# Batch 0 of an attention-and-feed-forward kernel: value projections ahead of the products, copies on two engines, a second block put off

## The chip, the cores and the metric

The kernel runs on one core of a Trainium2 chip. The metric is the device time of one execution in microseconds (us). Runs of this kernel on one core show a granted TensorE clock of 0.998 to 1.0. A ratio is computed as the mean time of one kernel's runs over that of the other's of the same rounds, so it is not quite the ratio of the medians that are quoted.

## The reference, cut to what matters

```python
# q, k, v: 8 batches x 8 heads x 1024 positions x 64; E, F: 64 x 1024
k_proj = einsum('ks,bhsd->bhkd', E, k)
v_proj = einsum('ks,bhsd->bhkd', F, v)
attn   = softmax(q @ k_proj^T / sqrt(64))          # over 64 projected keys
x      = (attn @ v_proj), heads side by side       # 8192 tokens x 512
h      = x @ w_in                                  # 512 -> 2048
out    = (h * clip(h + 3, 0, 6) / 6) @ w_out       # 2048 -> 512
```

The feed-forward part holds nearly all the matmul work: 2048 matmuls of 128*128 by 512 columns. Attention of batch b + 1 is woven into the feed-forward work of batch b. Batch 0 has nothing to hide behind: its attention is the head of the program.

## The kernel before

Heads go in pairs (`j`, four of them); tokens in two blocks (`t`, 512 each). Everything below is batch 0.

```python
def values_out(self, ps, hs, second=None, copies=(0, 1)):   # projected values: PSUM -> SBUF, twice
    src = ps[KP:].rearrange("p (h d) -> p h d", d=D)
    for a in copies:        # a = 0: rows 0-63, read by block 0; a = 1: rows 64-127, read by block 1
        (second if a and second else nc.vector.tensor_copy)(self.vp[a * KP:(a + 1) * KP, hs, :], src)

def quads(self, stationary, j, alloc, ts=range(NB)):        # sums and products: 64*64 tiles of the array
    tiles = {t: alloc() for t in ts}
    for t in ts:
        for a in range(2):
            r, c = t * KP, a * D                            # block t uses row half t
            nc.tensor.matmul(tiles[t][c:c + D]..., stationary(r, 2 * j + a), self.aT[j][r:r + KP, :, a, :], ...)
    return tiles

def by_pairs(self):
    ...
    for j in range(KO):                                     # the first loop
        keys(j)
        if j > 0: self.scores(j - 1, pmm)                   # ends in two exponentials on ScalarE
        busy(1)                                             # filler: one matmul nobody reads
        self.keys_transposed(2 * j, 2)
        self.q_out(j, self.q_transpose(j, pat))
        busy(1)
        if j > 0:
            ts = range(NB) if j == 1 else (0,)              # pair 0: both blocks
            den = self.sums(j - 1, pmm, ts)
            lns = {t: self.log(den[t]) for t in ts}         # 1 / sum = exp(-log(sum)), on ScalarE
            recs[j - 1, 0] = reciprocal(lns[0], opool, "o_sb")
            if j == 1:
                recs[0, 1] = self.inverse(lns[1])
            busy(1)
    self.scores(KO - 1, pmm)
    rest = []
    for j in range(KO):                                     # the tail
        copy = vals(j)                                      # eight projection matmuls
        copy(0)
        if j == 0: copy(1)
        else: rest.append(copy)
        av = self.values(j, pat, range(NB) if j == 0 else (0,))
        self.scaled(j, 0, av[0], recs[j, 0])
        busy(1)
        if j == 0:
            self.scaled(0, 1, av[1], recs[0, 1])
            den = self.sums(KO - 1, pmm, (0,))
            ...
            busy(1)
    for copy in rest: copy(1)
    busy(2)

def second_block(self):                  # one step after each feed-forward group
    for j in range(1, KO):
        for _ in range(3): yield
        den = self.sums(j, pat, (1,))[1]                    # "a visit"
        av = self.values(j, pat, (1,))[1]
        rec = self.inverse(self.log(den))
        yield
        self.scaled(j, 1, av, rec)
```

The softmax here doesn't subtract the row's maximum and nothing guards it: scores larger than these inputs give would overflow.

Of the kernel before, what the change touches and what calls it, by code (L numbers as in the profile page):

```python
# [15 lines left out]
def kernel(  # L16
# [11 lines left out]
    nc = tc.nc  # L28
# [7 lines left out]
    KO = d_model // P  # L36
    FO = d_ff // P
    TOK = 512
    NB = S // TOK
# [19 lines left out]
    opool = ctx.enter_context(tc.tile_pool(name="o", bufs=4))  # L59
# [5 lines left out]
    def pmm():  # L65
        return ps_mm.tile([P, TOK], f32, tag="mm", name="mm")

    def pat():
        return ps_at.tile([P, TOK], f32, tag="at", name="at")
# [11 lines left out]
    def busy(n):  # L81
        ps = pmm()
        for _ in range(n):
            nc.tensor.matmul(ps, ones[:, :P], ones, start=True, stop=True)  # L84
# [57 lines left out]
    class Attention:  # L142
# [15 lines left out]
            for a in range(2):  # L158
                (second if a and second else nc.vector.tensor_copy)(self.kp[:, hs, a, :], src)  # L159

        def values_out(self, ps, hs, second=None, copies=(0, 1)):
            src = ps[KP:].rearrange("p (h d) -> p h d", d=D)
            for a in copies:
                (second if a and second else nc.vector.tensor_copy)(self.vp[a * KP:(a + 1) * KP, hs, :], src)  # L164

        def keys_transposed(self, h0, n):
# [50 lines left out]
        def sums(self, j, alloc, ts=range(NB)):  # L217
            return self.quads(lambda r, h: ones[r:r + KP, :D], j, alloc, ts)
# [15 lines left out]
            nc.vector.tensor_mul(self.xT[:, j, t, :], av, rec)  # L234



        def by_pairs(self):
            def pair(j):
                return slice(2 * j, 2 * j + 2)  # L240

            def keys(j):
                pk = pat()[:, :P]
                for so in range(SO):
                    self.project(pk, 0, pair(j), so)
                self.keys_out(pk, pair(j))

            def vals(j):
                pv = pat()[:, :P]
                for so in range(SO):  # L250
                    self.project(pv, 1, pair(j), so)
                return lambda a: self.values_out(pv, pair(j), copies=(a,))

            def reciprocal(ln, pool, tag):
                rec = pool.tile([P, TOK], f32, tag=tag, name=tag)
                nc.scalar.activation(rec, ln, AF.Exp, scale=-1.0)
                return rec


            recs = {}  # L260
            for j in range(KO):
                keys(j)
                if j > 0:
                    self.scores(j - 1, pmm)
                busy(1)
                self.keys_transposed(2 * j, 2)
                self.q_out(j, self.q_transpose(j, pat))
                busy(1)
                if j > 0:
                    ts = range(NB) if j == 1 else (0,)  # L270
                    den = self.sums(j - 1, pmm, ts)
                    lns = {t: self.log(den[t]) for t in ts}
                    recs[j - 1, 0] = reciprocal(lns[0], opool, "o_sb")
                    if j == 1:
                        recs[0, 1] = self.inverse(lns[1])
                    busy(1)
            self.scores(KO - 1, pmm)
            rest = []
            for j in range(KO):
                copy = vals(j)  # L280
                copy(0)
                if j == 0:
                    copy(1)
                else:
                    rest.append(copy)
                av = self.values(j, pat, range(NB) if j == 0 else (0,))
                self.scaled(j, 0, av[0], recs[j, 0])
                busy(1)
                if j == 0:
                    self.scaled(0, 1, av[1], recs[0, 1])  # L290
                    den = self.sums(KO - 1, pmm, (0,))
                    recs[KO - 1, 0] = reciprocal(self.log(den[0]), opool, "o_sb")
                    busy(1)
            for copy in rest:
                copy(1)
            busy(2)


        def second_block(self):
            for j in range(1, KO):  # L300
                for _ in range(3):
                    yield
                den = self.sums(j, pat, (1,))[1]
                av = self.values(j, pat, (1,))[1]
# [3 lines that stand above are left out]
# [97 lines left out]
    second = first.second_block()  # L405
# [69 lines left out]
```

## Time and profile before

| | before |
|---|---|
| median of six runs | 522.02 us (521.97 to 522.26) |
| first key projection | 8.00 us |
| first feed-forward group of batch 0 | 27.79 us |
| first projection of batch 1 | 56.61 us |
| second-block visits | 3 |

In the lines of profiles below, PE is TensorE, PEld its weight loads, DVE is VectorE, ACT is ScalarE and POOL is GpSimd; a q behind the name is the engine's sequencer, and L373 is line 373 of that kernel's file. `mm` and `at` are PSUM tiles, `aT` the exponentials of a pair, `vp` its projected values, `xT` the scaled attention output. A bracket such as [0.70 <-ACT aT L203] says that the engine stood idle for 0.70 us before this line, and that ScalarE's exponentials ended the wait.

The last three rows are read from the instructions in order of time. The first key projection starts when the first loads (E and F) have landed and been turned; that moment wanders between 7.5 and 8.1 us from run to run, so later I subtract it. The difference "first projection of batch 1 minus first key projection" is the length of the part that the change touches: 56.61 - 8.00 = 48.61 us here.

### The profile page before, as it was taken

The numbers are of one execution on the slowest core, as the hardware profiler recorded it, in microseconds if no ns is written. First come the engines' busy times: TensorE is split into PE (matmuls) and PEld (weight loads), VectorE is DVE, ScalarE is ACT, GpSimd is POOL, SyncE is SP. The second block draws the span as 40 slices with busy tenths as digits, with TensorE's granted clock in tenths as the row PEclk, the third lists the DMA queues.
The fourth block names the chain that finished last, engine by engine and source line by source line (L and its number), as shares of the span: only waits on it lengthen the run. The fifth ranks groups of instructions, "written<-read, shape, count | busy, mean of one in ns | idle before, by whom it ended". The sixth has DMA issues, their size and how long they took to land.

```text
span 520.4 us, 7264 instructions
## 1 busy us (share of the span) xinstructions
PE 506.5 (97%) x2804; PEld 225.7 (43%) x2856; DVE 239.5 (46%) x379; ACT 284.0 (55%) x517; POOL 35.4 (7%) x53
## 2 busy tenths in 40 slices
PE   7899999999999999999999999999999999999997
PEld 3444444444444444444444444444444444444443
DVE  3478536444363453554454354534525544444420
ACT  2667485675446654568437664466635664444431
POOL 7520001000020000200002000200000000000000
PEclk9999999999999999999999999999999999999999
DMA  9999993993049611795119831298111110111112
GB/s 168 203 207 207 207 180 108 185 150 96 27 76 210 144 42 40 120 195 121 42 30 166 175 85 42 61 206 169 42 40 32 40 42 24 38 40 43 40 42 81
DMA packets 67443, 54.21 MB, mean 104 GB/s; under 512 B 29776, under 2 KB 59216, under 8 KB 67408
## 3 DMA queue, kind: packets, MB, share of 16 engines
q0 software_dynamic: 29856, 29.36, 35.0%
q1 hardware_dynamic: 37328, 23.99, 17.3%
q10 hardware_dynamic: 224, 0.39, 0.3%
q8 instruction: 22, 0.36, 0.3%
q14 instruction: 13, 0.11, 0.1%
HBM read 59.24 MB, written 16.78 MB: 146 GB/s over the span
## 4 chain that ended last, share of the span: by engine, by line
PE 94%; ACT 1%; DVE 1%; issue 1%; DMA 1%; DVEq 0%; ACTq 0%
PE mm L373 43%; PE mm L382 41%; PE at L212 4%; PE at L152 3%; PE at L198 1%; DMA ef_f<-in_F_dram 1%; PE mm L84 1%; PE at L182 1%; ACT aT L203 0%; PE mm L212 0%; DVE vp L164 0%; ACT ln L225 0%; PE mm L198 0%; DVE kp L159 0%; ACT rec L230 0%
## 5 line engine op out<-in xcount | busy, mean ns | idle before, releaser
L377 DVE SCALAR_TENSOR_TENSOR g<-r,mm 128x512 bf16<-128x512 f32 x256 | 173.2, 685 | 218.3 <-ACT r L376 218.1
L373 PE MATMUL mm<-xT,w_in_sb 128*128 128x512 bf16 x1000 | 233.1, 379 | 2.6 <-issue 1.9
L382 PE MATMUL mm<-w_out_sb,g 128*128 128x512 bf16 x999 | 230.1, 379 | 1.5 <-issue 0.3
L376 ACT ACTIVATE r<-mm 128x512 f32<-128x512 f32 x256 | 152.3, 603 | 66.1 <-PE mm L373 64.7
L373 PEld LDWEIGHTS <-w_in_sb 128*128 128x128 bf16 x1024 | 96.9, 98 | 125.5 <-issue 14.1
L382 PEld LDWEIGHTS <-g 128*128 128x128 bf16 x1024 | 99.0, 98 | 119.3 <-issue 2.2
L396 ACT COPY o_sb<-mm 128x512 f32<-128x512 f32 x63 | 36.9, 586 | 147.7 <-PE mm L382 144.8
L234 DVE TENSOR_TENSOR xT<-at,rec 128x512 bf16<-128x512 f32 x52 | 35.5, 683 | 15.4 <-ACT rec L230 15.4
L230 ACT ACTIVATE rec<-ln 128x512 f32<-128x512 f32 x60 | 38.0, 640 | 0.1
L225 ACT ACTIVATE ln<-at 128x512 f32<-128x512 f32 x59 | 32.6, 617 | 2.3 <-PE at L212 2.3
L203 ACT ACTIVATE aT<-at 128x512 bf16<-128x512 f32 x56 | 29.2, 612 | 0.9 <-PE at L198 0.9
L338 POOL COPY mark<-kT 1x1 bf16<-1x1 bf16 x5 | 0.9, 176 | 277.9 <-DMA kT<-kp 277.9
L152 PE MATMUL at<-k,ef_t 128*64 128x512 bf16 (+1 forms) x88 | 15.9, 324 | 0.3 <-issue 0.3
L152 PE MATMUL at<-v,ef_t 128*64 128x512 bf16 (+1 forms) x88 | 15.9, 324 | 0.0
L212 PE MATMUL at<-aT,vp 64*64 64x512 bf16 x112 | 12.6, 379 | 1.5 <-DVE vp L164 1.5
L152 PEld LDWEIGHTS <-ef_t 128*64 128x64 bf16 x176 | 9.5, 109 | 9.6 <-issue 4.7
L212 PE MATMUL at<-aT,ones 64*64 64x512 bf16 x118 | 12.7, 400 | 0.0
L164 DVE CAST vp<-at 64x512 bf16<-64x512 f32 (+1 forms) x21 | 11.2, 541 | 2.8 <-PE at L152 1.6
L84 PE MATMUL mm<-ones 128*128 128x512 bf16 x29 | 10.4, 440 | 1.6 <-DVE ones L77 1.5
L159 DVE CAST kp<-at 64x512 bf16<-64x512 f32 (+1 forms) x21 | 10.2, 523 | 3.1 <-PE at L152 3.0
L212 PEld LDWEIGHTS <-ones 64*64 64x64 bf16 x128 | 4.0, 103 | 14.8 <-issue 14.0
L189 DVE COPY qTp<-at 128x1024 bf16<-128x1024 bf16 x8 | 5.5, 691 | 7.5 <-PE at L182 7.5
(44 smaller groups left out, 100.4 us busy)
## 6 DMA issues: line engine op xcount, KB each, us to landing
out_dram<-o_sb SPq DMA_DIRECT2D x63, 256.0 KB, 2.0
q<-in_q_dram POOLq DMA_DIRECT2D x7, 1024.0 KB, 9.8
k<-in_k_dram POOLq DMA_DIRECT2D x7, 1024.0 KB, 15.3
v<-in_v_dram POOLq DMA_DIRECT2D x7, 1024.0 KB, 20.2
w_out_sb<-in_moe_w_out_dram POOLq DMA_DIRECT2D x4, 512.0 KB, 27.6
w_in_sb<-in_moe_w_in_dram POOLq DMA_DIRECT2D x3, 512.0 KB, 13.2
k<-in_k_dram POOLq DMA_DIRECT2D x4, 256.0 KB, 6.6
q<-in_q_dram POOLq DMA_DIRECT2D x4, 256.0 KB, 7.1
```

Source lines behind the costliest of these rows:

```text
L84: nc.tensor.matmul(ps, ones[:, :P], ones, start=True, stop=True)
L152: nc.tensor.matmul(ps[e * KP:(e + 1) * KP], ef_t[e][:, so, :], kqv[self.b]["kv"[e]][:, hs, so, :], start=(so == 0), stop=(so == SO - 1))
L203: nc.scalar.activation(self.aT[j][:, r].rearrange("p a n -> p (a n)"), tiles[r], AF.Exp, scale=scale)
L212: nc.tensor.matmul(tiles[t][c:c + D].rearrange("p (r n) -> p r n", r=2), stationary(r, 2 * j + a), self.aT[j][r:r + KP, :, a, :], start=Tr ...
L225: nc.scalar.activation(ln, den, AF.Ln)
L230: nc.scalar.activation(rec, ln, AF.Exp, scale=-1.0)
L234: nc.vector.tensor_mul(self.xT[:, j, t, :], av, rec)
L373: nc.tensor.matmul(h_ps, w_in_sb[:, ko, fo * P:(fo + 1) * P], xT[:, ko, t, :], start=(ko == 0), stop=(ko == KO - 1))
L376: nc.scalar.activation(r, h_ps, AF.Relu, bias=0.5, scale=1.0 / 6.0)
L377: nc.vector.scalar_tensor_tensor(g[:, fo, :], r, 1.0, h_ps, op0=ALU.min, op1=ALU.mult)
L382: nc.tensor.matmul(o_ps, g[:, fo, c * P:(c + 1) * P], w_out_sb[:, fo, :], start=(fo == 0), stop=(fo == FO - 1))
L396: nc.scalar.copy(o_sb, o_ps)
```

## The change

The intent: keep TensorE from standing still while a projection's copy is made, by issuing the next projection first; take the second copy off VectorE; and get pair 0's second block out of the head, into the feed-forward phase where the other pairs' second blocks already are.

```diff
             for j in range(KO):
                 keys(j)
 ...
                 if j > 0:
-                    ts = range(NB) if j == 1 else (0,)
-                    den = self.sums(j - 1, pmm, ts)
-                    lns = {t: self.log(den[t]) for t in ts}
-                    recs[j - 1, 0] = reciprocal(lns[0], opool, "o_sb")
-                    if j == 1:
-                        recs[0, 1] = self.inverse(lns[1])
+                    sums(j - 1)                      # block 0 only
                     busy(1)
             self.scores(KO - 1, pmm)
-            ... (the tail loop shown above)
+            vals(0)                                  # copies: VectorE, then ScalarE
+            vals(1)
+            sums(KO - 1)
+            products(0)                              # block 0 only, then its scaling
+            busy(1)
+            vals(2)
+            products(1)
+            busy(1)
+            products(2)
+            vals(3)
+            busy(1)
+            products(3)
+            busy(2)
 
         def second_block(self):
-            for j in range(1, KO):
-                for _ in range(3):
+            for j in range(KO):
+                for _ in range(2):
                     yield
```

More of the change, by code (lines that the diff above doesn't have):

```diff
@@ L159, in keys_out, with values_out @@
                 (second if a and second else nc.vector.tensor_copy)(self.kp[:, hs, a, :], src)
-        def values_out(self, ps, hs, second=None, copies=(0, 1)):
+        def values_out(self, ps, hs, second=None):
             src = ps[KP:].rearrange("p (h d) -> p h d", d=D)
-            for a in copies:
+            for a in range(2):
                 (second if a and second else nc.vector.tensor_copy)(self.vp[a * KP:(a + 1) * KP, hs, :], src)
@@ L251, in vals @@
                     self.project(pv, 1, pair(j), so)
-                return lambda a: self.values_out(pv, pair(j), copies=(a,))
+                self.values_out(pv, pair(j), nc.scalar.copy)
             def reciprocal(ln, pool, tag):
@@ L257, in reciprocal, with sums, products @@
                 return rec
-            recs = {}
+            one = (0,)
+            recs, avs = {}, {}
+            def sums(j):
+                ln = self.log(self.sums(j, pmm, one)[0])
+                recs[j] = reciprocal(ln, opool, "o_sb")
+            def products(j):
+                self.scaled(j, 0, self.values(j, pat, one)[0], recs[j])
             for j in range(KO):
@@ L269, in by_pairs @@
                 if j > 0:
-                    ts = range(NB) if j == 1 else (0,)
-                    den = self.sums(j - 1, pmm, ts)
-                    lns = {t: self.log(den[t]) for t in ts}
-                    recs[j - 1, 0] = reciprocal(lns[0], opool, "o_sb")
-                    if j == 1:
-                        recs[0, 1] = self.inverse(lns[1])
+                    sums(j - 1)
                     busy(1)
             self.scores(KO - 1, pmm)
-            rest = []
-            for j in range(KO):
-                copy = vals(j)
-                copy(0)
-                if j == 0:
-                    copy(1)
-                else:
-                    rest.append(copy)
-                av = self.values(j, pat, range(NB) if j == 0 else (0,))
-                self.scaled(j, 0, av[0], recs[j, 0])
-                busy(1)
-                if j == 0:
-                    self.scaled(0, 1, av[1], recs[0, 1])
-                    den = self.sums(KO - 1, pmm, (0,))
-                    recs[KO - 1, 0] = reciprocal(self.log(den[0]), opool, "o_sb")
-                    busy(1)
-            for copy in rest:
-                copy(1)
+            vals(0)
[10 more added lines that the diff above has]
+            products(3)
             busy(2)
         def second_block(self):
-            for j in range(1, KO):
-                for _ in range(3):
+            for j in range(KO):
+                for _ in range(2):
                     yield
```

## The prediction

> **What bounds the kernel now.** I read the shares of the engines first, then the chain that ended last, then the first 80 us in order of time, then who waited for whom.
>
> ```profile
> PE 506.5 (97%) x2804; PEld 225.7 (43%) x2856; DVE 239.5 (46%) x379; ACT 284.0 (55%) x517; POOL 35.4 (7%) x53
> PE 94%; ACT 1%; DVE 1%; issue 1%; DMA 1%; DVEq 0%; ACTq 0%
> ```
>
> TensorE is busy for 97% of the span and is 94% of the chain. From 27.79 us on, where batch 0's first feed-forward group starts, its waits add up to only a few us, and they hang on its own order of work. So the time is the start of that group, plus all matmul work after it. The change touches both: it reorders the head before 27.79 us and moves one matmul slot behind it. All gain must come from TensorE's idle time and filler before 27.79 us.
>
> Two stretches of that head carry the argument (columns: start us, duration us, engine, line, operation; in brackets idle time before it and what ended it):
>
> ```profile
> 12.37 0.41 PE L212 MATMUL mm<-aT,ones 64*64 64x512 bf16 x4
> 12.81 1.09 ACT L225 ACTIVATE ln<-mm 128x512 f32<-128x512 f32 x2 [0.50 <-PE mm L212]
> 13.78 0.63 ACT L256 ACTIVATE o_sb<-ln 128x512 f32<-128x512 f32 x1
> 14.30 0.63 ACT L230 ACTIVATE rec<-ln 128x512 f32<-128x512 f32 x1
> 14.82 1.08 ACT L203 ACTIVATE aT<-mm 128x512 bf16<-128x512 f32 x2
> 15.96 0.40 PE L212 MATMUL mm<-aT,ones 64*64 64x512 bf16 x2 [0.70 <-ACT aT L203]
> ```
>
> Pair 0 takes logarithm and reciprocal for both token blocks (four activations). The exponentials of pair 1, whose scores TensorE started at 13.59, wait behind them until 14.82, and TensorE then stands still for 0.70 us.
>
> ```profile
> 19.43 0.41 PE L198 MATMUL mm<-qTp,kT 64*64 64x256 bf16 x8 [0.25 <-DVE qTp L189]
> 20.38 1.06 ACT L203 ACTIVATE aT<-mm 128x512 bf16<-128x512 f32 x2
> 20.79 0.73 PE L212 MATMUL at<-aT,vp 64*64 64x512 bf16 x4 [0.39 <-DVE vp L164]
> 22.43 0.63 PE L152 MATMUL at<-v,ef_t 128*64 128x128 bf16 x8
> 23.10 0.29 DVE L164 CAST vp<-at 64x128 bf16<-64x128 f32 x1 [0.51 <-PE at L152]
> 23.45 0.40 PE L212 MATMUL at<-aT,vp 64*64 64x512 bf16 x2 [0.39 <-DVE vp L164]
> 27.79 3.62 PE L373 MATMUL mm<-xT,w_in_sb 128*128 128x512 bf16 x16
> PE at L212 <- DVE vp L164: 1.5, 4, 0.4
> ```
>
> In the tail each pair is projection, copy, product in strict sequence. Projection start to product start is 1.02 us, though the projection's eight matmuls free TensorE after 0.56 us (keys at 16.61, scores at 17.17). So 0.46 us is lost four times; the wait list shows 0.39 of each.
>
> The second block's price, after 27.79 us:
>
> ```profile
> 31.34 0.40 PE L212 MATMUL at<-aT,ones 64*64 64x512 bf16 x2
> 31.58 0.38 PE L212 MATMUL at<-aT,vp 64*64 64x512 bf16 x2
> 31.89 3.63 PE L373 MATMUL mm<-xT,w_in_sb 128*128 128x512 bf16 x16
> ```
>
> The starts 27.79, 31.89, 36.00 and 40.11 lie 4.10 to 4.11 us apart, and sixteen matmuls at 0.216 are 3.46. One second-block visit costs TensorE 0.64 us.
>
> **What the Trainium skill says.** "TensorEngine Tiling (Array Packing)", Key Properties: tiles of the array run independently, and changing the tiling mode drains TensorE. The trace agrees: four 64*64 matmuls of pair 0's sums took 0.41 us, two took 0.40, so dropping block 1's sums there saves TensorE nothing, and doing them later costs a new visit. "TensorE: Matmul & The Clock Gate", the engine queue depths in Part 1: ScalarE and VectorE are strict FIFOs. The trace agrees: pair 1's ready exponentials stood behind four activations. "PSUM — Partial Sum Buffer", Terms: two engines on one bank and quadrant at once are a collision, even both reading. The trace shows the program keeping to that: batch 1's key copies on the two engines run one after the other (VectorE 60.77 for 0.68, ScalarE only at 61.48, released by VectorE). So "two engines" will not make the pair of copies parallel; it only takes the second one off VectorE. "ScalarE: Activation LUTs", What ACT_TABLE_LOAD costs: 186 ns + 0.833 ns per element for an activation with immediates. For 512 elements that gives 613 ns, and the trace has 580 to 600; for the new copy of 128 elements it gives 0.29 us, an estimate.
>
> **The change part by part.**
>
> *1. Block 1 of pair 0 leaves the first loop.* TensorE: nothing (0.41 against 0.40). ScalarE loses one log and one reciprocal. Recomputed: log at 12.81, reciprocal 0.62 later (19.22 to 19.84 in the pair-3 case) at 13.43, ScalarE free 0.54 later at 13.97. Scores started at 13.59, and exponentials can follow 0.45 later (17.18 to 17.63), at 14.04. They end 1.08 later at 15.12, and pair 1's sums can start at 15.18. TensorE gets there at 14.88 + 0.31 = 15.19. So 15.20 instead of 15.96: **gain 0.76**. The next step (sums to sums 2.81 us) stays as it is, so pair 3's scores start at 18.67 and their exponentials end at 21.44 - 0.76 = 20.68.
>
> *2. The tail, step by step* (pitches from the trace: projection 0.56, products to filler 0.33, filler to next 0.32, sums to products in the same mode 0.24):
> - projection 0 at 19.01, projection 1 at 19.57, done 20.13. No copy is waited for.
> - sums of pair 3: need both exponentials, end 20.68, so 20.74. **New wait 0.61.**
> - products 0 at 20.98, filler 21.31, projection 2 at 21.63, products 1 at 22.19, filler 22.52, products 2 at 22.83 (copy of pair 2 on VectorE 22.30 to 22.59, then 0.06: in time), projection 3 at 23.16, filler 23.72, free at 24.04.
> - products 3: projection 3 done at 23.83, but VectorE is in the scaling of pair 2 (start 23.36 behind pair 1's, 0.66 each), so the copy runs 24.02 to 24.31 and products 3 start at 24.37. **Remaining wait 0.33.**
> - two fillers: 0.33 + 2 x 0.216 = 0.77 to the first group, at 25.14. The last scaling ends about 25.6; the matmul that reads it is the fourth, at 25.79.
>
> Tail before: 27.79 - 19.77 = 8.02. After: 25.14 - 19.01 = 6.13. **Gain 1.89.** Its terms: waits 1.84 become 0.94 (0.90); block 1 of pair 0's products, which came one after the other (0.66 to the filler), leaves 0.33; one single filler and one of the last three go (about 0.54); the rest is cheaper mode changes.
>
> *3. Copies.* Products of block 0 read only the half that VectorE copies. ScalarE's copies stand behind the pair 3 exponentials (two from 20.68) and end before its logarithm can start at 21.18 or just after; the reciprocal is needed only near 24.9. The three late copies that VectorE had at 28.03 lay beside matmuls and are worth nothing.
>
> *4. Second block.* Four visits instead of three: **loss 0.64**. Every three groups instead of four: ScalarE needs 3 x 0.54 + 1.2 = 2.8 us and VectorE 4 x 0.66 = 2.6 us of each 3 x 0.864 + 0.64 = 3.23 us, so neither becomes the bound.
>
> Sum: 522.11 - 0.76 - 1.89 + 0.64 = **520.1 us**.
>
> **The rivals.**
> - *Value loads become the bound.* The table of DMA issues gives 11.1, 11.1, 11.0 and 11.0 us to landing; from issues at 7.57, 8.31, 9.63 and 10.88 the four pairs land at 18.67, 19.41, 20.63 and 21.88. My times of need are 19.01, 19.57, 21.63 and 23.16. All arrive before, the second by only 0.16, and behind it comes a 0.61 wait which would swallow that. If they came 1 us late, the time would be 520.6 to 521. Nothing in the change reorders loads, so I give this little.
> - *The earlier start is lost to a later load.* Weight pieces land at 23.26, 24.63, 27.15, 29.70 and 32.2; the fifth group would need the third piece at 29.2. The last piece of the second weights lands at 29.94 + 27.6 = 57.5; its use moves from 62.8 to 60.8. Batch 2's values land at 42.86 + 31.8 = 74.7, needed at 81.0 - 2.0 = 79.0. Nothing becomes late; if something did, 522.1.
> - *Second-block visits crowd ScalarE.* After a visit the next activation is about 0.35 us late and has caught up two groups later; three groups suffice by my sum. If PSUM backed up at each visit, add 0.3 x 4: 521.3.
> - *The new order is a pure win without the exponential wait*, if ScalarE reached pair 3 sooner: at most 0.6 better, 519.5. Against it speaks the strict order of log, reciprocal, exponentials on ScalarE.
>
> **Range and chances.** The three terms have errors of perhaps 0.3 each from pitches read to 0.05 us, and runs spread by 0.3 (521.97 to 522.26). Losses are likelier than extra gains, as every new order of engines can uncover a wait. So 519.5 to 521.0. 2% is 10.4 us, far more than the head's whole idle time; within 2% has 0.987, faster 0.008, slower 0.005.
>
> **What would show it.** Right: no 0.70 us idle before pair 1's sums near 15.2; a wait of about 0.6 on the exponentials before pair 3's sums at 20.7; one wait near 0.3 on the value copy before the last products; first group near 25.1; four second-block visits about 3.2 us apart; the rest shifted by 2.0 us. Wrong: TensorE waiting on a value load, the first products waiting for ScalarE's copy, or matmul gaps between second-block visits.

## More of the kernel before

A warning on one number. This is the costliest TensorE group of the page (columns: line, engine, operation, tiles, shapes and count; then busy time and mean ns; then idle time before it and its releaser):

```profile
L373 PE MATMUL mm<-xT,w_in_sb 128*128 128x512 bf16 x1000 | 233.1, 379 | 2.6 <-issue 1.9
```

The program has 1024 of these matmuls, not 1000: some records are missing from this trace, and each gap shows as idle time that ended by itself ("issue"). So the share of TensorE is a lower bound, and small "issue" gaps are not waits.

## The result, and the profile after

The changed kernel takes 520.14 us (median of six runs, 520.02 to 520.19) against 522.02 us: 1.88 us less. The ratio is 0.9963 with a 95% interval from 0.9950 to 0.9976: a real gain of 0.4%, within 2%. The prediction was 520.1.

The page of the changed kernel: shares of the engines, the chain that ended last, and the costliest TensorE group (the feed-forward line is now line 370):

```profile
PE 511.5 (99%) x2854; PEld 225.5 (44%) x2854; DVE 238.6 (46%) x375; ACT 285.2 (55%) x521; POOL 35.4 (7%) x53
PE 96%; DVE 1%; ACT 1%; issue 0%; DVEq 0%; ACTq 0%
L370 PE MATMUL mm<-xT,w_in_sb 128*128 128x512 bf16 x1024 | 236.6, 379 | 0.0
```

TensorE's busy time seems to have risen by 5 us in a kernel that does less. It has not: this trace has all 1024 records, and the 2.6 us of idle time ahead of that group are gone with the gaps. Shares of busy time cannot measure this change; start times can.

The first loop around pair 1 (in order of time, columns as in the prediction):

```profile
12.14 0.40 PE L212 MATMUL mm<-aT,ones 64*64 64x512 bf16 x2 
12.59 0.60 ACT L225 ACTIVATE ln<-mm 128x512 f32<-128x512 f32 x1 [0.50 <-PE mm L212]
13.21 0.63 ACT L255 ACTIVATE o_sb<-ln 128x512 f32<-128x512 f32 x1 
13.82 1.08 ACT L203 ACTIVATE aT<-mm 128x512 bf16<-128x512 f32 x2 
14.96 0.40 PE L212 MATMUL mm<-aT,ones 64*64 64x512 bf16 x2 
```

One logarithm and one reciprocal stand ahead of the exponentials, and pair 1's sums start without a wait. On the clock of the first key projection (7.77 here, 8.00 before) they come at 7.19 instead of 7.96.

The tail:

```profile
18.77 1.11 PE L152 MATMUL at<-v,ef_t 128*64 128x128 bf16 x16 
19.38 1.06 ACT L203 ACTIVATE aT<-mm 128x512 bf16<-128x512 f32 x2 
20.50 0.40 PE L212 MATMUL mm<-aT,ones 64*64 64x512 bf16 x2 [0.61 <-ACT aT L203]
...
22.45 1.35 DVE L234 TENSOR_TENSOR xT<-at,o_sb 128x512 bf16<-128x512 f32 x2 
...
23.82 0.29 DVE L164 CAST vp<-at 64x128 bf16<-64x128 f32 x1 
24.15 0.26 ACT L164 CAST vp<-at 64x128 bf16<-64x128 f32 x1 [1.53 <-DVE vp L164]
24.17 0.40 PE L212 MATMUL at<-aT,vp 64*64 64x512 bf16 x2 [0.30 <-DVE vp L164]
24.95 2.75 PE L370 MATMUL mm<-xT,w_in_sb 128*128 128x512 bf16 x12 
```

Sixteen projection matmuls (pairs 0 and 1) run on almost without a stop (0.04 us, see the rivals below); the exponentials of pair 3 then make TensorE wait 0.61 us; two scalings keep VectorE until 23.8, and the last products wait 0.30 us for the copy behind them. From first projection to first group the tail is 24.95 - 18.77 = 6.18 us, against 8.02 before. ScalarE's copy of a pair does wait for VectorE's copy of the same tile, and the products do not wait for it.

The first second-block visit after it:

```profile
27.63 0.40 PE L212 MATMUL at<-aT,ones 64*64 64x512 bf16 x2 
27.87 0.38 PE L212 MATMUL at<-aT,vp 64*64 64x512 bf16 x2 
28.19 2.76 PE L370 MATMUL mm<-xT,w_in_sb 128*128 128x512 bf16 x12 
```

Visits start at 27.63, 30.88, 34.13 and 37.37, 3.24 to 3.25 us apart, with twelve matmuls of 0.216 us (2.59) between: 0.65 us a visit, four times. From there on every output copy of the changed kernel lies 2.17 to 2.18 us ahead of the kernel before, to the last one. 0.23 of that is the wandering start; 1.95 is the change.

### The profile page after: what moved, and what is told of

It is laid out like the page before. It is cut to its first block, busy times and chain, and to the rows that moved or that the text cites. A ratio compares the mean times of both kernels' runs of the same rounds, so it can differ in the third digit from the quotient of the medians.

```text
span 518.3 us, 7310 instructions
## 1 busy us (share of the span) xinstructions
PE 511.5 (99%) x2854; PEld 225.5 (44%) x2854; DVE 238.6 (46%) x375; ACT 285.2 (55%) x521; POOL 35.4 (7%) x53
## 4 chain that ended last, share of the span: by engine, by line
PE 96%; DVE 1%; ACT 1%; issue 0%; DVEq 0%; ACTq 0%
PE mm L370 44%; PE mm L379 42%; PE at L212 3%; PE at L152 3%; PE mm L84 2%; PE at L198 1%; PE at L182 1%; PE mm L212 0%; ACT aT L203 0%; DVE xT L234 0%; PE mm L198 0%; DVE kp L159 0%; DVE vp L164 0%; ACT ln L225 0%; PE at L169 0%
## 5 line engine op out<-in xcount | busy, mean ns | idle before, releaser
L370 PE MATMUL mm<-xT,w_in_sb 128*128 128x512 bf16 x1024 | 236.6, 379 | 0.0
L84 PE MATMUL mm<-ones 128*128 128x512 bf16 x30 | 11.7, 477 | 1.5 <-DVE ones L77 1.5
```

What stands on the lines that cost most here:

```text
L84: nc.tensor.matmul(ps, ones[:, :P], ones, start=True, stop=True)
L370: nc.tensor.matmul(h_ps, w_in_sb[:, ko, fo * P:(fo + 1) * P], xT[:, ko, t, :], start=(ko == 0), stop=(ko == KO - 1))
```

## The experiments

Eleven runs, all correct, five rounds each (four runs for combined_recip) beside the kernel before on the same chip (whose median there was 522.01 to 522.05). The table gives the median of the runs, and from the profiled run the "touched part" (first projection of batch 1 minus first key projection, 48.61 before). The two columns of differences need not agree to better than about 0.2 us, because the median also carries the wandering start; in free_block and combined, the end of the program adds some 0.35 us, as told there.

Every kernel of the table is within 2% of the kernel before. The 95% intervals of the ratios reach some 0.7 us to either side. Those of late_recip (0.9978 to 1.0003) and put_off_only (0.9980 to 1.0007) include 1, all others lie below it. So the gains of these two, and every difference of a few tenths between two of the new kernels, rest on the start times in the profiled runs and not on the times alone.

| kernel | median us | less than before | touched part us | less than before |
|---|---|---|---|---|
| changed kernel | 520.14 | 1.88 | 54.43 - 7.77 = 46.66 | 1.95 |
| late_recip | 521.45 | 0.56 | 55.87 - 7.78 = 48.09 | 0.52 |
| put_off_only | 521.60 | 0.41 | 56.30 - 8.08 = 48.22 | 0.39 |
| order_only | 520.52 | 1.49 | 54.91 - 7.77 = 47.14 | 1.47 |
| copies_vector | 520.35 | 1.66 | 54.77 - 7.93 = 46.84 | 1.77 |
| no_fillers | 519.62 | 2.43 | 53.79 - 7.53 = 46.26 | 2.35 |
| sums_later | 519.65 | 2.40 | 53.94 - 7.51 = 46.43 | 2.18 |
| free_block | 519.83 | 2.22 | 53.85 - 7.78 = 46.07 | 2.54 |
| free_block_again | 519.79 | 2.23 | 53.87 - 7.79 = 46.08 | 2.53 |
| combined | 518.72 | 3.30 | 52.73 - 7.78 = 44.95 | 3.66 |
| combined_padded | 518.33 | 3.71 | 52.72 - 7.89 = 44.83 | 3.78 |
| combined_recip | 517.82 | 4.22 | 52.10 - 7.55 = 44.55 | 4.06 |

The theory throughout is that of the prediction: ScalarE's strict order makes the wait in the first loop, copies make the waits in the tail, a visit costs TensorE 0.64 us. The main rivals are that one of the two parts (put-off or new order) makes the whole gain, and that the second engine matters.

### late_recip: one reciprocal moved in the kernel before

```diff
                     self.scores(j - 1, pmm)
+                    if j == 2:
+                        recs[0, 1] = self.inverse(ln01)
 ...
-                        recs[0, 1] = self.inverse(lns[1])
+                        ln01 = lns[1]
```

> The kernel before, with one activation moved: the reciprocal of pair 0's second block is issued behind pair 1's exponentials instead of ahead of them; nothing else changes. Theory (ScalarE's strict order causes the 0.70 us wait of pair 1's sums): exponentials start when the first reciprocal frees ScalarE, 0.50 us earlier than before (14.32 instead of 14.82), sums 0.50 us earlier, time 522.02 - 0.50 = 521.5. Rival (the wait belongs to TensorE's own earlier work, or is given back by the later reciprocal standing before pair 1's logarithm): 522.0.

Measured: 521.45 us. The order of time:

```profile
14.08 1.08 ACT L203 ACTIVATE aT<-mm 128x512 bf16<-128x512 f32 x2 
15.03 0.65 ACT L230 ACTIVATE rec<-ln 128x512 f32<-128x512 f32 x1 
15.21 0.40 PE L212 MATMUL mm<-aT,ones 64*64 64x512 bf16 x2 [0.18 <-ACT aT L203]
```

With nothing but one activation behind instead of ahead of the exponentials, the wait of pair 1's sums fell from 0.70 to 0.18 us, and the time by as much. The wait was made by the order of ScalarE's queue. It is also the cheapest lesson: half a microsecond for moving one line, about as much as the whole put-off earns net.

### put_off_only: the put-off without the new order

```diff
-                    ts = range(NB) if j == 1 else (0,)
+                    ts = (0,)
 ...
-                av = self.values(j, pat, range(NB) if j == 0 else (0,))
+                av = self.values(j, pat, (0,))
 ...
-            for j in range(1, KO):
-                for _ in range(3):
+            for j in range(KO):
+                for _ in range(2):
```

> The kernel before with only pair 0's second block put off (four visits in the feed-forward phase); the order of value projections and products and the engine of the copies stay. Theory: exponentials' wait -0.76, products of pair 0 halved -0.33, one visit more +0.64, together -0.45: 521.6, no wait of pair 1's sums, tail still with four waits of about 0.4 on copies. Rival (the put-off is what pays, the order of the tail is worth little): about 520.5. Second rival (put-off costs a visit and gains nothing): 522.7.

Measured: 521.60 us. Pair 1's sums start without a wait, 7.19 us after the first key projection (15.27 - 8.08), as in the changed kernel:

```profile
15.27 0.40 PE L212 MATMUL mm<-aT,ones 64*64 64x512 bf16 x2
```

The tail keeps its waits of 0.38 to 0.39 us on copies. Pair 0's products reach the filler after them in 0.33 us (20.10 to 20.43) instead of 0.66. Gain and price of the put-off nearly cancel: it pays for its extra visit and 0.4 us more.

### order_only: the new order without the put-off

```diff
             def sums(j):
+                ts = range(NB) if j == 0 else one
 ...
             def products(j):
+                av = self.values(j, pat, range(NB) if j == 0 else one)
 ...
-            for j in range(KO):
-                for _ in range(2):
+            for j in range(1, KO):
+                for _ in range(3):
```

> The changed kernel with pair 0's second block taken back into the head (three visits); the order of value projections ahead of products and the copies on two engines stay. Theory: the 0.70 us wait of pair 1's sums is back, tail gain 1.89 less 0.35, because VectorE's extra scaling (0.66) stands before the copy of pair 2's and pair 3's values: 522.02 - 1.54 = 520.5. Rival (the put-off is needed for most of the gain): 521.5 or more.

Measured: 520.52 us. The wait of 0.70 us in the first loop is back. VectorE's extra scaling is where it was expected:

```profile
22.61 0.68 DVE L234 TENSOR_TENSOR xT<-at,rec 128x512 bf16<-128x512 f32 x1
23.32 0.29 DVE L164 CAST vp<-at 64x128 bf16<-64x128 f32 x1
...
23.67 0.40 PE L212 MATMUL at<-aT,vp 64*64 64x512 bf16 x2 [0.16 <-DVE vp L164]
```

It pushes pair 2's copy, and pair 2's products now wait. Four fifths of the change's gain (1.49 of 1.88) come with the new order and the copies on two engines, and the put-off adds 0.4 on top of either order. The rival that the put-off makes the gain falls. Not tested: this kernel with late_recip's moved reciprocal. If that gave its 0.5 us here too, the put-off and its fourth visit would not be needed; this is an estimate from the two runs.

### copies_vector: both copies on VectorE

```diff
-                self.values_out(pv, pair(j), nc.scalar.copy)
+                self.values_out(pv, pair(j))
```

> The changed kernel with both copies of each value projection on VectorE. Theory: only pair 2's second copy delays anything (it pushes the scalings of pairs 1 and 2 by about 0.2, they push pair 3's first copy and so the last products): +0.2, 520.3. Rival A (second engine worthless): 520.1. Rival B (each second copy on VectorE costs its whole 0.3 us on the path): 520.7 or more.

Measured: 520.35 us, 0.2 us more than the changed kernel, and the wait of the last products grew from 0.30 to 0.48 us. The 0.2 agrees with the theory and with the touched part (0.18), but the runs spread from 519.99 to 520.59, so the times alone would not separate it from nothing. Rival B, 0.6 us, falls.

### no_fillers: the tail without its filler matmuls

The five `busy` matmuls between `vals(0)` and the end of `by_pairs` are left out.

> The changed kernel without the five filler matmuls of the tail (three single ones and the last two). Theory: the first filler and the last two stand where TensorE waits for nothing; without them products 1 come 0.32 earlier, VectorE's chain of copies and scalings becomes the bound (products 3 at 23.8 on the changed profile's clock instead of 24.17), and the first group's fourth matmul then waits about 0.3 for pair 3's scaling: gain about 0.5, 519.6. Rival A (fillers lie in waits anyway): 520.1. Rival B (without them the granted clock falls): slower than 520.1, with a clock below 1.0 in the head.

Measured: 519.62 us, at a granted clock of 1.00 in the first 26 us. Of the five matmuls' 1.08 us (five times 0.216) 0.40 came out of the touched part. The wait of the last products grew from 0.30 to 0.68 us: VectorE is now the bound there.

```profile
23.70 0.40 PE L212 MATMUL at<-aT,vp 64*64 64x512 bf16 x2 [0.68 <-DVE vp L164]
```

Fillers in a gap cost nothing; those that stood outside a gap cost 0.4 to 0.5 us and bought nothing that these runs show.

### sums_later: work into the wait for the exponentials

```diff
             vals(1)
-            sums(KO - 1)
             products(0)
-            busy(1)
             vals(2)
+            sums(KO - 1)
+            busy(1)
             products(1)
```

> The changed kernel with products 0 and value projection 2 ahead of pair 3's sums, and the first filler after these sums, so that the 0.61 us wait for the exponentials is filled with work. Theory: that wait goes, but pair 2's values land only near 20.5 on the changed profile's clock, so projection 2 now waits about 0.3 for its load, and VectorE's scalings of pairs 1 and 2 still stand before the last copy: gain 0.25, 519.9. Rival A (the wait is simply filled): gain 0.6, 519.5. Rival B (VectorE's chain sets the last products regardless): 520.1.

Measured: 519.65 us. The touched part fell by 0.23 us, as expected. The median fell by 0.49, which is nearer to rival A's 519.5; the profiled run's early start (7.51 against 7.77) makes up the difference there, and rival A's picture, a wait that is simply filled, is not what the profile shows. The new bound showed where it was expected, a transfer:

```profile
20.25 0.61 PE L152 MATMUL at<-v,ef_t 128*64 128x128 bf16 x8 [0.30 <-DMA v<-in_v_dram]
```

In the changed kernel pair 2's values landed at 20.48 (issue at 9.87, 10.6 us to landing) and their projection started at 21.37, so that order left this load 0.89 us of room; the earlier projection uses it up.

### free_block: pair 0's second block beside other work, not put off

```diff
+            def beside():
+                quad(ones_of, KO - 1, 0, s3)      # pair 3's sums, block 0: row half 0
+                quad(ones_of, 0, 1, s0)           # pair 0's sums, block 1: row half 1
+                quad(vp_of, 0, 0, a0)
+                quad(vp_of, 0, 1, a1)
+                ... logarithms, reciprocals and scalings
 ...
-            for j in range(KO):
-                for _ in range(2):
+            for j in range(1, KO):
+                for _ in range(3):
```

> The changed kernel with pair 0's second block computed in the tail: its sums together with pair 3's sums, its products together with pair 0's first products, in the array's other row half; logarithm and reciprocal behind pair 3's on ScalarE, scaling on VectorE between the copy of pair 3's values and the last scaling; three visits later instead of four; the last fillers share one PSUM tile. Theory: the four 64*64 matmuls in other quadrants cost TensorE nothing, a whole visit (0.64) goes: 519.5. Rival A (second-block matmuls cost TensorE the same wherever they stand): 520.1. Rival B (the scaling on VectorE or the held PSUM tile delays the first group): 519.8 to 520.3, with a wait at the first group.

Measured: 519.83 us, where 519.5 was expected. The number lies in rival B's range, but its sign, a wait at the first group, is not there: that group starts at 25.03, 0.08 us later than in the changed kernel. The four sums matmuls in two row halves took TensorE 0.41 us, as two did:

```profile
20.50 0.41 PE L268 MATMUL mm<-aT,ones 64*64 64x512 bf16 x4 [0.65 <-ACT aT L203]
```

The touched part fell by 0.59 us, so the work of the visit was nearly free. All output copies were 0.56 to 0.58 us ahead of the changed kernel's, but the last one only 0.20. The VectorE half of that last copy, first in the changed kernel, then here:

```profile
514.63 0.42 DVE L388 COPY o_sb<-mm 128x256 f32<-128x256 f32 x1 [16.00 <-PE mm L379]
```

```profile
514.43 0.42 DVE L411 COPY o_sb<-mm 128x256 f32<-128x256 f32 x1 [16.37 <-PE mm L402]
q14 instruction: 1, 0.01, 0.2%
```

VectorE idled 0.37 us longer before its last instruction. The second line, from the list of DMA queues of the last 14 us, is one packet on an instruction queue there; the profiles of the changed kernel and of the runs above have none in that stretch.

> The very kernel of the run with pair 0's second block in the other row half, again. There the trace put every output copy 0.56 to 0.58 us ahead of the changed kernel's, except the last, which was only 0.20 ahead; the time was 519.83 where 519.5 was expected. If those 0.37 us at the very end belong to this program, they come again and the median is 519.8; if they were a chance of that chip or run, the last copy is 0.57 ahead too and the median is 519.5 to 519.6.

Measured: 519.79 us, the same idle time (16.36) and the same packet. It belongs to the program.

### combined: what the runs pointed to

```diff
             vals(0)
             vals(1)
-            sums(KO - 1)
             products(0)
-            busy(1)
             vals(2)
-            products(1)
-            busy(1)
+            sums of pair 3, block 0, and of pair 0, block 1
+            products of pair 1, block 0, and of pair 0, block 1
             products(2)
-            vals(3)
-            busy(1)
+            vals(3), first copy on ScalarE, second on VectorE
             products(3)
-            busy(2)
```

> What the runs so far point to, put together: the changed kernel with products 0 and value projection 2 ahead of pair 3's sums, no fillers in the tail, pair 0's second block in the other row half (its sums beside pair 3's, its products beside pair 1's), three later visits, and the first copy of pair 3's values on ScalarE so that it doesn't stand behind VectorE's scalings. Theory: first group about 23.3 on the clock of the run with the later sums (24.46 there), a visit less: 518.0. It should start no earlier, as the first weight piece lands near 23.3. Rival A (the pieces hide each other and VectorE's chain still sets the last products): 519.0. Rival B (the second weight piece, some 1.3 us behind the first, or the third stops the feed-forward phase, with DMA waits on TensorE): 518.3 to 519.

Measured: 518.72 us. It beats both kernels, but is 0.7 us worse than expected. One part is again the last copy (1.70 us ahead of the changed kernel's until then, 1.35 for the last, with the packet). The other is my own slip: I had put pair 3's copy on ScalarE behind its logarithm and reciprocal, where it could not start before 23.06:

```profile
23.06 0.26 ACT L164 CAST vp<-at 64x128 bf16<-64x128 f32 x1
...
23.37 0.40 PE L212 MATMUL at<-aT,vp 64*64 64x512 bf16 x2 [0.89 <-ACT vp L164]
```

This run changes several things at once, so it shows what they bring together and not what each brings. The slip is the very mistake of the kernel before: ready work behind unready or unhurried work in a queue that keeps its order.

### combined_padded and combined_recip: the two causes one by one

```diff
+    pad = consts.tile([P, 1], bf16, name="pad")
+    for _ in range(4):
+        nc.vector.memset(pad, 0.0)
```

> The combined kernel with four one-column clears on VectorE added in the first two us, where VectorE waits for the first load, so that VectorE has 379 instructions instead of 375 and its instruction stream lies differently. Theory (the 0.35 us ahead of the very last output copy, seen in the three profiles in which one packet on an instruction queue falls after 512 us, is VectorE's last instruction being fetched): the packet is gone from the last 5 us, the last copy keeps the lead of the others, 518.72 - 0.35 = 518.4. Rival (the loss has another cause): 518.7.

Measured: 518.33 us, with the four instructions more. VectorE's last idle time is back at 16.00 us, the last copy is as far ahead as the others (1.70), and the packet has moved to between 495 and 500 us:

```profile
512.93 0.42 DVE L404 COPY o_sb<-mm 128x256 f32<-128x256 f32 x1 [16.00 <-PE mm L395]
```

So four more instructions ahead of it on VectorE decide over 0.35 us at the end of the program. That the late copy was waiting to be fetched, as the expectation has it, is not shown: the packet cannot have brought it. It starts at 515.1 in free_block and 514.2 in combined, 0.7 and 0.9 us after the copy's start (514.43 and 513.28). The traces' records of VectorE's semaphore waits, which the views leave out, show more. In the padded kernel a pause of 0.40 us (496.27 to 496.67) stands between two such waits that lie 0.05 us apart in combined, and the packet follows it, at 497.3. The changed kernel has the same pause at 503.51 to 503.91 and its packet at 504.6. In both the pause lies within VectorE's 16 us of idle time and costs nothing; in free_block and combined the 0.36 us fall right before the last copy. That it is a break between blocks of the instruction stream is likely, but only argued.

```diff
-            recs[KO - 1] = reciprocal(self.log(s3), opool, "o_sb")
+            ln3 = self.log(s3)
 ...
             vals(3, nc.scalar.copy, None)
+            recs[KO - 1] = reciprocal(ln3, opool, "o_sb")
```

> The padded combined kernel with pair 3's reciprocal issued behind ScalarE's copy of pair 3's values instead of ahead of it. In the combined kernel's profile that copy started at 23.06, when the reciprocal freed ScalarE, though its values were ready near 22.5, and the last products waited 0.89 us for it. Theory: products 3 at about 22.8, then the first group waits for its first weight piece (landing near 23.3 to 23.4) or its fourth matmul for the scaling near 24.1: 0.35 less than the padded one, 518.0. Rival (weights or the later reciprocal give it all back): 518.4.

Measured: 517.82 us (four runs, 517.69 to 517.96), ratio 0.9919 to the kernel before, interval 0.9906 to 0.9933. This is the best version. Against the padded kernel the touched part fell by 0.28 us and the median by 0.51; the profiled runs' starts (7.55 against 7.89) differ by more than the rest. The last products wait 0.35 us instead of 0.89:

```profile
22.57 0.40 PE L215 MATMUL at<-aT,vp 64*64 64x512 bf16 x2 [0.35 <-ACT vp L167]
```

After them the weight load of the first group waits 0.27 us for the first weight piece and its matmuls 0.15 us for the last scaling. The head now runs into its loads, so more reordering of it would probably gain little; no run tests this.

## Why the prediction was right, point by point

- **The bound.** TensorE's order of work from the first group on: shown. The lead of 2.18 us at batch 1 is the lead of every later output copy to the end of the program, within 0.01.
- **Part 1, the first loop, 0.76 predicted.** Measured 0.77 (7.96 to 7.19). That ScalarE's order is the cause is shown by late_recip, which moved one activation and won back 0.52, and by put_off_only, which took both away and reached the same 7.19 without the new order.
- **Part 2, the tail, 1.89 predicted.** Measured 8.02 - 6.18 = 1.84. All steps came in their order and place: the new wait on pair 3's exponentials 0.61 (0.61 predicted), the wait on the last copy 0.30 (0.33), the first group, set on the clock of before, at 24.95 + 0.23 = 25.18 (25.14). Of the missing 0.05, 0.03 had come by the time of the last products: the two scalings ahead of their copy took 1.37 (22.45 to 23.82) where the prediction counted 2 x 0.66.
- **Part 3, the copies.** That the second copy waits for the first, and that products do not wait for it, is in the profile. The prediction gave the second engine no figure; copies_vector puts it at 0.2 us. The prediction's estimate of 0.29 us for ScalarE's copy, from the Trainium skill's page "ScalarE: Activation LUTs", section What ACT_TABLE_LOAD costs, was a little high: the copy took 0.26, and two in a row 0.42.
- **Part 4, the fourth visit, 0.64 predicted.** Measured 0.65, and no matmul gap follows a visit at the closer spacing, so the rival of a crowded ScalarE falls. That the price is one of place and not of work is shown by free_block, where the same matmuls cost some 0.06 us (a visit of 0.65 less, but only 0.59 gained) and the filler behind them starts 0.07 us later (21.12 against 21.05).
- **Sum.** 0.76 + 1.89 - 0.64 = 2.01 predicted; 1.95 in the touched part, 1.88 between the medians. The rest is within the wandering start. That 520.1 lies only 0.04 from the median is in part luck: the sum starts from 522.11, the median of the three runs known then. From the later median of six, 522.02, it gives 520.01, which is 0.13 off. The three terms, each within 0.05, are the better test.
- **The rivals.** Late value loads: the prediction left pair 1's load 0.16 us of room, and it had none. It counted 0.56 us from the first projection to the second, the pitch to a group of another kind; without a wait the step is 0.47 (free_block, order_only). Pair 1's values landed at 19.23 in the changed kernel and the step was 0.51, so the load was 0.04 us late, and 0.14 in no_fillers (step 0.61). As the prediction said, the wait for the exponentials behind it swallowed that. A later load that eats the gain: no, the lead stays to the end. No exponential wait: it came as predicted.

## What to carry to other kernels

Before you issue an activation early "because its input is ready", look at what stands behind it in that engine's queue and who waits for that; moving one reciprocal was worth half a microsecond in late_recip, and 0.28 us of the touched part in combined_recip. When a transfer of results between engines makes TensorE wait, put the next independent group between producer and consumer, then ask which engine or load the new order will meet next: here exponentials, then VectorE's scalings, then a value load, then a weight piece. Small matmuls that use half of the array's rows are nearly free beside others of the same mode, and cost 0.65 us when they interrupt the full-size stream.

## What the Trainium skill lacked or had wrong

- "Runtime: NRT & Kernel Launch", section Instruction fetch mechanics, says that the cost of crossing a block boundary of the instruction stream is mostly hidden. In free_block and combined VectorE's last instruction came 0.36 to 0.37 us late, all of it in the time, with a packet on an instruction queue behind it; four early instructions moved both away. If this is such a crossing, which the runs don't prove, it isn't hidden when it falls on the last instruction.
- "TensorEngine Tiling (Array Packing)", Key Properties, says that a change of tiling mode drains the array, but gives no price. Here four 64*64 matmuls between full-size groups cost 0.64 to 0.65 us, the change of mode and their own work together, and 0.06 us beside others of their mode.
- No page that I read says that matmul records can be missing from a trace. The one before had 1000 of 1024 for one line and so 1.9 us of idle time marked "issue"; the one after had all 1024. A comparison of busy shares (97% and 99%) was worthless.
